# Activations split per head pair, six single-tile chunks and query lows on GpSimd: one change to a fused attention and expert kernel

## Chip, cores and metric

The kernel runs on one core of a Trainium2 chip. The metric is the time of one launch in microseconds (us) on the device: the median of three runs before the change is 1324.6 us.

## The reference

Top-k attention over q, k, v of shape (4, 8, 576, 64), then two expert layers over the 2304 rows of 512 that it leaves. All is float32.

```python
scores = scale * np.matmul(q, k.transpose(0, 1, 3, 2))
kth = np.partition(scores, -32, axis=-1)[..., -32:-31]
scores = np.where(scores >= kth, scores, -1e9)
attn = softmax(scores)                      # over the 32 that are kept
x = (attn @ v) as (2304, 512)
x = (sigmoid(x @ w_gate) * (x @ w_val)) @ w_out     # 512 -> 1536 -> 512
out = relu(x @ w_in) ** 2 @ w_out2                  # 512 -> 2048 -> 512
```

## The kernel before

The 2304 rows are 18 tiles of 128 rows. Attention works on a *unit*: one tile and one head, so 8 units to a tile and 144 in all; a head pair `hp` is two heads of a tile, four pairs to a tile. The expert layers work on *chunks* of one or two tiles (`CHUNKS`, line 30): tiles 0 to 3 alone, then seven pairs. All matrices are wanted at nearly float32 accuracy: the experts' operands are split into a high and a low float16 part and multiplied in three terms; chunk 0 alone (`PLAIN`) is multiplied in float32 while the weights are still being converted.

A unit runs so. `Pair.queries` (302) transposes a pair's queries on TensorE (PE) into PSUM; ScalarE (ACT) copies the high part out and VectorE (DVE) subtracts it to get the low part (line 320). `scores` (325) multiplies them with the keys and ACT copies the result to `S` (347). `softmax` (350) finds the 32 largest of a row with four MAX8 and three MATCH_REPLACE8 on DVE (358, 364), GpSimd (POOL) makes the biases `bs`, and ACT masks and exponentiates. Then there are two ways, parted by `TCI` (65). Chunks below it normalise on POOL, transpose the probabilities on PE (`transpose`, 430) and multiply them with float32 values (`values`, 508). Chunks from it on keep two float16 parts of the probabilities (ACT 386 and 387, POOL 391 and 394), turn them with a transposing DMA (410) and multiply them with float16 values on PE (`values16`, 468). The values for that are prepared once for each batch and head pair: `prep_values` and `split_values` (186, 210) scale them by a power of two, kept in `vsc`, and write them to memory as two parts.

`values16` ends with a float32 product on POOL into the chunk's `xt` (504). When a chunk has all four head pairs, `split_x` (695) takes its norm (ACT square, four matmuls with ones into `pq`, a reduction and `pow2_scale` on DVE), scales it to the high part `xs[0]` on ACT (692) and makes the low part in two POOL passes (701, 702). Only then may the chunk's gate and value matmuls (738) run. They are followed by w_out (778), a second such split (805 to 820), w_in (841) and w_out2 (862).

The weights are converted and split in the first part (`conv`, `split`): the low part of every `LOP`-th block is made on POOL (652, 653), of the others on DVE (650).

The order on each engine is set ahead by a scheduler from priorities and dependences; the engines then run their queues in order. `attend` (1121) emits units ahead of the expert steps, by `LEAD` units for chunks below `PRE0` and by `LEAD2` after it; from `PRE0` on the next chunk's first gate and value blocks (`NPRE`) are put ahead of the present chunk's second layer. Within attention, `head(n + 1)` (1016) emits loads, queries and scores of the next unit, and `tail` (1050) the values of an earlier one. `add_manual_dep` ties an instruction behind another for the order alone.

## Time and profile before

| what | value |
|---|---|
| median of 3 runs | 1324.6 us (1322.24 to 1328.76) |
| the profiled execution | 1327.31 us, of which the span from its first to its last instruction is 1325.5 us |
| PE (matmuls) busy | 1190.7 us, 90% |
| DVE busy | 999.0 us, 75% |
| POOL busy | 809.7 us, 61% |
| ACT busy | 807.8 us, 61% |
| mean granted PE clock | 0.942 of full |

Busy times are unions over the span; PE's contain matmuls whose ends are modelled. The shares are means over a first part with weight conversion and attention, a middle with attention and experts, and an end with experts alone. Tile names in rows are the program's: `S` scores, `W` work copy, `PT` turned probabilities, `xp` the value product, `xs` the parts of x, `qt` queries, `pg`, `pv`, `acc`, `ph` the experts' accumulators.

### The profile page before, as it was taken

To read this page: it belongs to the slowest core of one execution; us is meant where nothing else is said; L and a number is where in the kernel's file an instruction comes from. 1 tells how busy PE (TensorE), PEld (TensorE's weight loads), DVE (VectorE), ACT (ScalarE), POOL (GpSimd) and SP (SyncE) were. 2 spreads that over 40 slices of the span, in tenths; PEclk is the share of its full clock that TensorE was granted. 3 is DMA by queue.
4 is the path that set the end of the run, shared out by engine and by line. 5 is a ranking of instruction groups with operands and counts; after the bars stand their busy time and mean duration, and the time that the engine had idled before them with its cause. 6 is when DMAs were issued, how large, how long until landed. Compare 5 with 4: busy or idle time off the path is not lost.

```text
span 1325.5 us, 30239 instructions
## 1 busy us (share of the span) xinstructions
PE 1190.7 (90%) x11357; PEld 947.1 (71%) x11357; DVE 999.0 (75%) x2040; ACT 807.8 (61%) x1584; POOL 809.7 (61%) x1324
## 2 busy tenths in 40 slices
PE   6756999977989879889986999999999999999998
PEld 5544886865868758756874768877886887787775
DVE  6999996897899989887989777878999899210010
ACT  4777786776666676656666665656677657323122
POOL 1798868867566576557556764575657647424223
PEclk9658999979999979979996999999999999999999
DMA  7988851233356454656745255556444333100000
GB/s 196 330 285 293 269 178 28 77 100 101 102 120 144 115 129 98 147 115 155 179 109 128 72 128 136 123 124 152 100 100 108 97 82 65 44 1 1 17 1 16
DMA packets 263409, 157.95 MB, mean 119 GB/s; under 512 B 213344, under 2 KB 229728, under 8 KB 263264
## 3 DMA queue, kind: packets, MB, share of 16 engines
q1 hardware_dynamic: 263264, 156.03, 45.4%
q8 instruction: 89, 1.46, 0.5%
q14 instruction: 56, 0.46, 0.1%
HBM read 103.55 MB, written 19.40 MB: 93 GB/s over the span
## 4 chain that ended last, share of the span: by engine, by line
PE 54%; POOL 11%; DVE 10%; DMA 8%; ACT 8%; issue 6%; SPq 2%; ACTq 0%; POOLq 0%; DVEq 0%
PE ph L841 12%; PE acc L862 11%; PE pg L738 7%; PE pv L738 6%; PE acc L778 6%; PE sp L344 5%; DMA PT<-S 3%; DVE mx L358 3%; DVE W L364 3%; PE xp L482 3%; POOL S L391 2%; ACT W L387 1%; DMA kst<-ks 1%; ACT W L376 1%; ACT S L386 1%
## 5 line engine op out<-in xcount | busy, mean ns | idle before, releaser
L358 DVE MAX8 mx<-W 128x8 f32<-128x576 f32 x432 | 327.5, 758 | 10.5
L841 PE MATMUL ph<-x,wi_w 128*128 128x256 f16 (+1 forms) x1920 | 207.6, 262 | 7.1 <-ACT x L817 6.3
L364 DVE MATCH_REPLACE8 W<-mx,W 128x576 f32<-128x576 f32 x288 | 213.7, 742 | 0.0
L391 POOL TENSOR_TENSOR S<-W,S 128x512 f16<-128x512 f32 x112 | 130.0, 1160 | 128.7 <-ACT W L387 127.6
L862 PE MATMUL acc<-w_w,rh 128*128 128x512 f16 x816 | 194.8, 380 | 4.0 <-POOL rh L854 4.0
L841 PEld LDWEIGHTS <-wi_w 128*128 128x128 f16 x1920 | 167.9, 100 | 41.5 <-issue 9.9
L376 ACT ACTIVATE W<-S,bs 128x576 f32<-128x576 f32 x144 | 111.6, 775 | 106.7 <-POOL bs L372 106.2
L344 PE MATMUL sp<-kst,qt 128*128 128x288 f32 x608 | 139.2, 337 | 25.7 <-ACT S L347 14.5
L738 PE MATMUL pg<-xs,wg_w 128*128 128x256 f16 (+1 forms) x1440 | 157.7, 261 | 2.8 <-POOL xs L702 2.0
L738 PE MATMUL pv<-xs,wv_w 128*128 128x256 f16 (+1 forms) x1440 | 153.1, 258 | 1.2 <-ACT th L748 0.6
L738 PEld LDWEIGHTS <-wg_w 128*128 128x128 f16 x1440 | 124.6, 99 | 21.4 <-issue 3.7
L862 PEld LDWEIGHTS <-rh 128*128 128x128 f16 x816 | 77.1, 98 | 82.6 <-POOL rh L854 5.9
L347 ACT COPY S<-sp 128x576 f32<-128x576 f32 x144 | 91.6, 636 | 72.9 <-DMA PT<-S 36.3
L778 PEld LDWEIGHTS <-wo_w 128*128 128x128 f16 x1440 | 123.0, 99 | 17.9 <-issue 5.1
L738 PEld LDWEIGHTS <-wv_w 128*128 128x128 f16 x1440 | 123.1, 99 | 16.7 <-issue 3.4
L778 PE MATMUL acc<-gh,wo_w 128*128 128x256 f16 (+1 forms) x1200 | 123.4, 255 | 4.6 <-POOL gh L754 2.8
L344 PEld LDWEIGHTS sp<-kst,qt 128*128 128x128 f32 x608 | 93.6, 196 | 43.7 <-ACT S L347 20.0
L750 DVE TENSOR_TENSOR th<-pv,th 128x512 f32<-128x512 f32 (+1 forms) x60 | 36.2, 604 | 111.4 <-PE pv L738 105.1
L853 POOL TENSOR_TENSOR r<-r 128x512 f32<-128x512 f32 (+1 forms) x80 | 74.5, 932 | 72.7 <-ACT rh L852 66.3
L358 DVE MAX8 mx<-S 128x8 f32<-128x576 f32 x144 | 107.0, 743 | 9.4 <-ACT S L347 9.4
L364 DVE MATCH_REPLACE8 W<-mx,S 128x576 f32<-128x576 f32 x144 | 106.9, 742 | 0.0
L386 ACT ACTIVATE S<-W,bs 128x576 f16<-128x576 f32 x112 | 86.7, 775 | 19.5 <-POOL bs L380 15.7
(336 smaller groups left out, 2172.1 us busy)
## 6 DMA issues: line engine op xcount, KB each, us to landing
kst<-ks SPq DMA_DIRECT2D x104, 288.0 KB, 3.1
v<-vd SPq DMA_DIRECT2D x40, 320.0 KB, 3.2
qn<-in_q_dram SPq DMA_DIRECT2D x128, 64.0 KB, 2.3
wi_r<-in_moe_w_in_dram SPq DMA_DIRECT2D x16, 512.0 KB, 6.6
w_r<-in_moe_w_out_dram SPq DMA_DIRECT2D x16, 512.0 KB, 4.9
wg_r<-in_moe_w_gate_dram SPq DMA_DIRECT2D x12, 512.0 KB, 6.5
wv_r<-in_moe_w_val_dram SPq DMA_DIRECT2D x12, 512.0 KB, 6.9
wo_r<-in_moe_w_out_dram SPq DMA_DIRECT2D x12, 512.0 KB, 6.0
```

Source lines behind the costliest of these rows:

```text
L344: nc.tensor.matmul(sp[:, e, 0:HALF], l, r, start=(x == 0), stop=(x == len(ops) - 1))
L347: nc.scalar.copy(ss.rearrange("p (e s) -> p e s", e=2), sp[:, :, 0:HALF])
L358: m8 = nc.vector.max(mx[:, r], cur)
L364: nc.vector.match_replace(wk, mx[:, r], cur, NEG)
L376: nc.scalar.activation(wk, ss, AF.Prelu, bias=bs[:, 0:1], scale=1.0, alpha=BIG)
L386: nc.scalar.activation(pp[:, 0:S], wk, AF.Exp, bias=bs[:, 1:2], scale=SCALE)
L391: nc.gpsimd.tensor_tensor(pp[:, S + ST : 2 * S], wk[:, 0:SM], pp[:, 0:SM], op=ALU.subtract)
L738: nc.tensor.matmul(pp[:, e * N : (e + 1) * N], wblk(wd, a, c, f0, P), xs[:, b_, c, :], start=(e == 0 and n == 0), stop=(n == 3 * KM - 1), ...
L778: nc.tensor.matmul(acc[:, d // 2, (d % 2) * N : (d % 2 + 1) * N], wblk("wo", a, f, d * P, P), gh[:, b_, e * N : (e + 1) * N], start=(f == ...
L841: nc.tensor.matmul(ph[:, e * N : (e + 1) * N], wblk("wi", a, c, f0, P), x2[:, b_, c, :], start=(e == 0 and n == 0), stop=(n == 3 * KM - 1) ...
L853: nc.gpsimd.tensor_tensor(r, r, r, op=ALU.mult)
L862: nc.tensor.matmul(acc2[:, i, 0:DM], gh[:, b_, e * N + i * P : e * N + (i + 1) * P], wblk("w2", a, f, 0, DM), start=(f == 0 and x == 0), s ...
```

## The change

Tiles 4 and 5 become chunks of their own, so there are twelve chunks, of which six are single; `TCI` is 6, so tiles 4 and 5 now take PE's transposes and float32 values, and batch 0's values are no longer prepared. For chunks from `TCI` on there is no `split_x`: the scale of the values is carried into the normalisation by `xfac`, one factor for each batch and head pair against a common scale of the chunk, and `values16` writes each head pair's product directly as two float16 parts: POOL product, ACT copy, POOL subtraction. The low part of the queries is made by POOL, from a second ACT copy of the transposed queries into `qn`. `LOP` 3 puts eleven of 34 weight lows on POOL where eight were. `LEAD` is 9 for 5, `PRE0` 6 for 5 (the same tiles). For chunks from `TCI` on, the next unit's `head` is emitted behind the present unit's MAX8 rows, without raised priority, and the reciprocal of the sums is tied to the second of them. Keys are prepared together with a batch's values. `ve` moves to another tag, and `mx` has two buffers for three.

```diff
-CHUNKS = [[0], [1], [2], [3]] + [[i, i + 1] for i in range(4, 18, 2)]
+CHUNKS = [[0], [1], [2], [3], [4], [5]] + [[i, i + 1] for i in range(6, 18, 2)]
-LEAD = 5
+LEAD = 9
-PRE0 = 5
+PRE0 = 6
-LOP = 4
+LOP = 3
-TCI = 4
+TCI = 6
...
-        ve = apool.tile([P, 2, D], F32, tag="qn", bufs=2, name=f"ve_{n}")
+        ve = apool.tile([P, 2, D], F32, tag="we", bufs=3, name=f"ve_{n}")
...
+    def xfac(ci, b):
+        if ci not in xfacs:
+            bs_ = batches(ci)
+            vf = vsc.bitcast(F32)
+            ix = mpool.tile([P, 1], F32, tag="xsc", bufs=3, name=f"ix_{ci}")
+            nc.vector.reduce_max(ix, vf[:, bs_[0] * NHP : (bs_[-1] + 1) * NHP, 1], axis=AX.X)
+            nc.gpsimd.tensor_scalar(ix, ix, 2.0, None, op0=ALU.mult)
+            fs = {}
+            for b_ in bs_:
+                f = mpool.tile([P, NHP], F32, tag="xfc", bufs=4, name=f"xfc_{ci}_{b_}")
+                nc.gpsimd.tensor_scalar(
+                    f, vf[:, b_ * NHP : (b_ + 1) * NHP, 0], ix, 1.0, op0=ALU.mult, op1=ALU.mult
+                )
+                fs[b_] = f
+            xfacs[ci] = ix, fs
+        return xfacs[ci][1][b]
...
                     nc.scalar.copy(qt[:, 0, :, sl], p3[:, :, sl])
-                    nc.vector.tensor_tensor(
-                        qt[:, 1, :, sl], p3[:, :, sl], qt[:, 0, :, sl], op=ALU.subtract
+                    whole = qn.rearrange("p j a d -> p j (a d)")[:, :, sl]
+                    nc.scalar.copy(whole, p3[:, :, sl])
+                    nc.gpsimd.tensor_tensor(
+                        qt[:, 1, :, sl], whole, qt[:, 0, :, sl], op=ALU.subtract
                     )
...
-            mx = apool.tile([P, TOPK // 8, 8], F32, tag="mx", bufs=3, name=f"mx_{tt}_{h}")
+            mx = apool.tile([P, TOPK // 8, 8], F32, tag="mx", bufs=2, name=f"mx_{tt}_{h}")
...
-                            vsc.bitcast(F32)[o : o + n, b * NHP + self.hp, 0:1],
+                            xfac(self.ci, b)[o : o + n, self.hp : self.hp + 1],
...
-            nc.gpsimd.tensor_tensor(
-                self.xt[:, self.hp, i * P : (i + 1) * P], xr[:, 0:P], xr[:, P : 2 * P], op=ALU.mult
-            )
+            xf = xr[:, 0:P]
+            nc.gpsimd.tensor_tensor(xf, xf, xr[:, P : 2 * P], op=ALU.mult)
+            hi, lo = (self.xt[:, a, self.hp, i * P : (i + 1) * P] for a in range(2))
+            nc.scalar.copy(hi, xf)
+            nc.gpsimd.tensor_tensor(lo, xf, hi, op=ALU.subtract)
...
+                    if (b, pr.hp) not in done:
+                        done.add((b, pr.hp))
+                        prep_keys(b, pr.hp)
...
-            with tc.high_priority(offset=int(up[0])):
-                head(n + 1)
-                if n > 0 and units[n - 1][0].ci < TCI:
-                    tail(n - 1)
-                if pr.ci >= TCI - 2:
-                    def late(mark, n=n):
-                        while late_values:
-                            split_values(*late_values.pop(0), mark)
-                        if units[n - 2][0].ci >= TCI:
-                            tail(n - 2, mark)
+            if pr.ci < TCI:
+                with tc.high_priority(offset=int(up[0])):
+                    head(n + 1)
+                    if n > 0 and units[n - 1][0].ci < TCI:
+                        tail(n - 1)
+            if pr.ci >= TCI - 2:
+                def late(marks, n=n, pr=pr):
+                    if pr.ci >= TCI:
+                        head(n + 1)
+                        if units[n - 1][0].ci < TCI:
+                            tail(n - 1)
+                    while late_values:
+                        split_values(*late_values.pop(0), marks[3])
+                    if units[n - 2][0].ci >= TCI:
+                        tail(n - 2, marks[3], marks[1])
```

What it does to the order shows best where the chunk of tiles 8 and 9 passes from attention to the experts. On PE before, the last value product `xp_3` is followed by the norm `x_6pq`, the next queries and scores, and only then by the first gate matmul on `xs` (the last number of a name is a buffer's):

```order
L494 MATMUL xp_3_10046<-ident,z_3_9663 64x128 x2
L688 LDWEIGHTS ones
L688 MATMUL x_6pq<-xs_10081,ones 128x256
...
L307 MATMUL qpt_1_10198<-ident,qn_1_9745 128x128 x2
L307 MATMUL qpt_1_10306<-ident,qn_1_9748 128x128 x2
L344 MATMUL sp_2_10335<-kst_2_2_9919,qt_1_2_10201 128x288 x4
L738 LDWEIGHTS wg_w_1877
L738 MATMUL pg_0_10444<-xs_10081,wg_w_1877 128x256
```

On PE now, nine gate and nine value matmuls on the first three head pairs (`xs_9479`), scores and the end of the chunk ahead (`acc_6`) stand before that last value product:

```order
L766 LDWEIGHTS wg_w_1885
L766 MATMUL pg_0_11130<-xs_9479,wg_w_1885 128x256
...
L766 MATMUL pv_0_11131<-xs_9479,wv_w_1895 128x256
L368 MATMUL sp_1_10861<-kst_1_2_10430,qt_0_2_10384 128x288 x4
L766 LDWEIGHTS wv_w_1895
...
L806 LDWEIGHTS wo_w_2023
L806 MATMUL acc_6_10507<-gh_5_10964,wo_w_2023 128x256
L508 LDWEIGHTS v_3_2_9833
L508 MATMUL xp_3_10716<-PT_6_10313,v_3_2_9833 64x128
```

The norm's rows are gone, and the gate matmuls have moved from behind the last head pair to ahead of it.

On DVE before, in the same place, between the MAX8 and MATCH_REPLACE8 rows of a unit:

```order
L364 MATCH_REPLACE W_1_10341<-mx_1_10342,S_1_10191 128x576
L690 TENSOR_REDUCE x_6cm<-x_6pq 128x1
L358 MAX mx_1_10342<-W_1_10341 128x8
L129 TENSOR_SCALAR x_6sn<-x_6cm 128x1
L364 MATCH_REPLACE W_1_10341<-mx_1_10342,W_1_10341 128x576
L132 TENSOR_SCALAR x_6s<-x_6sn 128x1
L135 TENSOR_SCALAR x_6s<-x_6sn 128x1
L320 TENSOR_TENSOR qt_1_2_10201<-qpt_1_10198,qt_1_2_10201 128x256
L358 MAX mx_1_10342<-W_1_10341 128x8
```

On DVE now, the unit whose scores follow the first gate matmuls:

```order
L383 MAX mx_1_10968<-S_1_10860 128x8
L390 MATCH_REPLACE W_1_10967<-mx_1_10968,S_1_10860 128x576
L383 MAX mx_1_10968<-W_1_10967 128x8
L499 RECIPROCAL z_0_10612<-z_0_10612 128x2
L390 MATCH_REPLACE W_1_10967<-mx_1_10968,W_1_10967 128x576
L383 MAX mx_1_10968<-W_1_10967 128x8
```

The reduction, the scale steps and the query lows have left DVE's queue.

On POOL before, the chunk's product is followed by a unit's biases and lows and then by the two passes over the whole chunk:

```order
L504 TENSOR_TENSOR xt_8962<-xr_3_10078 128x128
L372 TENSOR_SCALAR bs_0_10213<-mx_0_10205 128x1
L373 TENSOR_SCALAR bs_0_10213<-mx_0_10205 128x1
L380 TENSOR_SCALAR bs_0_10213<-bs_0_10213 128x1
L391 TENSOR_TENSOR S_0_10030<-W_0_10204,S_0_10030 128x512
L394 TENSOR_TENSOR S_0_10030<-W_0_10204,S_0_10030 128x64
L221 MEMSET voe_2_10848 64x2x64
L701 TENSOR_SCALAR xt_8962<-xt_8962,x_6s 128x1024
L702 TENSOR_TENSOR xs_10081<-xt_8962,xs_10081 128x1024
```

On POOL now, two query lows and a unit's biases stand between the product of the last head pair and its low part:

```order
L531 TENSOR_TENSOR xr_3_10748<-xr_3_10748 128x128
L344 TENSOR_TENSOR qt_1_2_10870<-qn_1_10422,qt_1_2_10870 128x256
L398 TENSOR_SCALAR bs_0_10874<-mx_0_10852 128x1
L399 TENSOR_SCALAR bs_0_10874<-mx_0_10852 128x1
L344 TENSOR_TENSOR qt_1_2_10979<-qn_1_10425,qt_1_2_10979 128x256
L406 TENSOR_SCALAR bs_0_10874<-bs_0_10874 128x1
L534 TENSOR_TENSOR xs_9479<-xr_3_10748,xs_9479 128x128
```

The passes over 1024 columns became one of 128 columns for each head pair and tile, and the query lows came in between.

## Rows read from the trace of the kernel before

**Rows 1.** Page, part 2: busy tenths of an engine in 40 slices.
```profile
PE   6756999977989879889986999999999999999998
DVE  6999996897899989887989777878999899210010
```

**Rows 2.** Windows: length, busy us (instructions) of PE, PEld, DVE, ACT, POOL; clock, DMA, GB/s.
```profile
0.00:361.00 361.00, 288.35 (x2593) 238.94 (x2594) 315.34 (x601) 255.33 (x519) 256.04 (x329) 0.88 0.57 178
361.00:687.00 326.00, 294.38 (x3241) 236.27 (x3240) 286.06 (x612) 214.88 (x441) 202.60 (x405) 0.95 0.57 132
687.00:729.00 42.00, 25.58 (x243) 19.65 (x241) 36.13 (x83) 26.74 (x52) 26.86 (x52) 0.74 0.51 125
729.00:1134.00 405.00, 398.83 (x3813) 311.96 (x3814) 347.56 (x715) 262.65 (x495) 259.89 (x473) 0.99 0.47 106
1134.00:1325.50 191.50, 183.55 (x1475) 140.25 (x1473) 13.94 (x34) 48.17 (x78) 64.25 (x68) 0.99 0.04 12
```

**Rows 3.** Windows of line 358 alone, the MAX8 rows on DVE.
```profile
0.00:361.00 361.00, 93.67 (x129) 0.88 0.57 178
361.00:687.00 326.00, 142.75 (x194) 0.95 0.57 132
687.00:1134.00 447.00, 190.69 (x256) 0.97 0.47 108
```

**Rows 4.** Timeline, 706 to 721 us: start, us, what, [idle before, releaser].
```profile
706.62 0.46 POOL L504 TENSOR_TENSOR xt<-xr 128x128 f32<-128x128 f32 x1
...
708.22 1.01 PE L688 MATMUL x_6pq<-xs,ones 128*128 128x256 bf16 x4 [6.41 <-ACT xs L685]
...
713.22 1.13 POOL L701 TENSOR_SCALAR xt<-xt,x_6s 128x1024 f32<-128x1024 f32 x1
714.43 2.13 POOL L702 TENSOR_TENSOR xs<-xt,xs 128x1024 f16<-128x1024 f32 x1
...
717.99 2.69 PE L738 MATMUL pg<-xs,wg_w 128*128 128x256 f16 x23
```

**Rows 5.** DVE's waits, 0 to 687, then 687 to 1134: us, times, longest.
```profile
DVE qt L320 <- ACT qt L319: 8.5, 7, 3.1
...
DVE qt L320 <- ACT qt L319: 21.6, 12, 7.0
```

**Rows 6.** Groups by shape, whole span: count, busy us, mean ns, idle before.
```profile
L320 DVE TENSOR_TENSOR qt<-qpt,qt 128x256 fp32r<-128x256 f32 x64 | 26.6, 416 | 14.4 <-ACT qt L319 13.8
L650 DVE SCALAR_TENSOR_TENSOR wi_w<-wi_c,wis,wi_w 128x1024 f16<-128x1024 f32 x7 | 12.4, 1770 | 0.4 <-ACT wi_w L647 0.4
L853 POOL TENSOR_TENSOR r<-r 128x256 f32<-128x256 f32 x24 | 16.2, 680 | 4.6 <-ACT rh L852 3.9 <-ACT vs L205 0.2
L482 PE MATMUL xp<-PT,v 128*64 128x64 f16 x448 | 12.0, 199 | 0.0
L482 PE MATMUL xp<-PT,v 128*64 128x128 f16 x1344 | 54.4, 230 | 4.7 <-DMA PT<-S 4.7
L494 PE MATMUL xp<-ident,z 128*64 128x128 f32 x224 | 23.6, 291 | 0.5 <-DVE z L473 0.5
L445 PE MATMUL tp<-ident,W 128*128 128x128 f32 x64 | 11.2, 301 | 2.3 <-POOL W L427 2.2
L518 PE MATMUL xp<-PT,v 128*64 128x128 f32 x256 | 22.6, 333 | 2.4 <-ACT PT L446 2.3
L518 PE MATMUL xp<-PE,v 64*64 64x128 f32 x64 | 8.6, 326 | 0.0
L841 PE MATMUL ph<-x,wi_w 128*128 128x128 f16 x576 | 41.0, 226 | 3.7 <-ACT x L817 3.0 <-ACT r L850 0.8
L841 PE MATMUL ph<-x,wi_w 128*128 128x256 f16 x1344 | 166.6, 278 | 3.3 <-ACT x L817 3.3
```

**Rows 7.** Timelines of PE: w_in matmuls in one go, 128 and 256 columns.
```profile
465.57 1.50 PE L841 MATMUL ph<-x,wi_w 128*128 128x128 f16 x24
...
1195.62 8.02 PE L841 MATMUL ph<-x,wi_w 128*128 128x256 f16 x72
```

More of the change, by code (lines that the diff above doesn't have):

```diff
@@ L253, in tile_topk_attention__then__two_moe_layers @@
     last_max = []
+    xfacs = {}
+    def xfac(ci, b):
[14 more added lines that the diff above has]
+        return xfacs[ci][1][b]
     class Pair:
@@ L354, in softmax @@
             wk = apool.tile([P, S], F32, tag="W", bufs=3, name=f"W_{tt}_{h}")
-            mx = apool.tile([P, TOPK // 8, 8], F32, tag="mx", bufs=3, name=f"mx_{tt}_{h}")
+            mx = apool.tile([P, TOPK // 8, 8], F32, tag="mx", bufs=2, name=f"mx_{tt}_{h}")
             cur = ss
+            marks = []
             for r in range(TOPK // 8):
@@ L362, in softmax @@
                     )
+                marks.append(m8.ins)
                 if r < TOPK // 8 - 1:
@@ L367, in softmax @@
             if late is not None:
-                late(m8.ins)
+                late(marks)
             bs = apool.tile([P, 4], F32, tag="bs", bufs=3, name=f"bs_{tt}_{h}")
@@ L466, in transpose, with values16 @@
                 nc.scalar.copy(self.pe[:, i * P : (i + 1) * P], tq[:, 0:P])
-        def values16(self, i, after=None):
+        def values16(self, i, after=None, summed=None):
             tt = self.tts[i]
@@ L473, in values16 @@
             rc = nc.vector.reciprocal(z, z)
-            if after is not None:
-                tc.add_manual_dep(rc.ins, after.name, NOSYNC, reason="summed by then")
+            if summed is not None:
+                tc.add_manual_dep(rc.ins, summed.name, NOSYNC, reason="summed by then")
             terms = [(a, c, c) for c in range(CB + 1) for a in range(2)]
@@ L1048, in head, with tail @@
                 nxt.queries(nxt.tts[0:1])
-        def tail(n, after=None):
+        def tail(n, after=None, summed=None):
             pr, pi, j, i = units[n]
@@ L1054, in tail @@
             if pr.hp == 0 and pr.ci not in xts:
-                if pr.ci in XP:
+                if pr.ci >= TCI:
+                    xts[pr.ci] = mpool.tile(
+                        [P, 2, KM, pr.N], F16, tag="m4", bufs=M4, name=f"xs_{pr.ci}"
+                    )
+                elif pr.ci in XP:
                     if not plain:
@@ L1073, in tail @@
             if pr.ci >= TCI:
-                pr.values16(i, after)
+                pr.values16(i, after, summed)
             else:
@@ L1080, in tail @@
                 if pr.hp == NHP - 1:
-                    xsp[pr.ci] = pr.xt if pr.ci in PLAIN else split_x(pr.ci, pr.xt)
+                    if pr.ci in PLAIN:
+                        xsp[pr.ci] = pr.xt
+                    elif pr.ci < TCI:
+                        xsp[pr.ci] = split_x(pr.ci, pr.xt)
+                    else:
+                        xsp[pr.ci] = pr.xt, xfacs[pr.ci][0]
         head(0)
@@ L1085, in attention @@
             late = None
-            with tc.high_priority(offset=int(up[0])):
-                head(n + 1)
-                if n > 0 and units[n - 1][0].ci < TCI:
-                    tail(n - 1)
-                if pr.ci >= TCI - 2:
-                    def late(mark, n=n):
-                        while late_values:
-                            split_values(*late_values.pop(0), mark)
-                        if units[n - 2][0].ci >= TCI:
-                            tail(n - 2, mark)
+            if pr.ci < TCI:
[5 more added lines that the diff above has]
+                def late(marks, n=n, pr=pr):
+                    if pr.ci >= TCI:
+                        head(n + 1)
[5 more added lines that the diff above has]
+                        tail(n - 2, marks[3], marks[1])
             work[n] = pr.softmax(j, i, ready.pop(n), late)
```

## Prediction

> **What bounds the kernel now.** I read the page's slices first, then the windows, then single waits and prices. In the slices VectorE (DVE) stands at 7 to 9 tenths until slice 34 of 40, at 9 mostly in the first 14, and falls to 0 to 2 after it, while TensorE (PE) has its holes in the first 22 slices and is full afterwards [rows 1]. The windows give this in microseconds [rows 2]. The attention of a 128-row tile is 8 heads ("units") of four MAX8 and three MATCH_REPLACE8 on DVE, in order. The MAX8 rows, four to a unit (129, 194 and 256, those on a bound counted twice), put the end of unit 32 (tiles 0 to 3) at 361 us, of unit 80 (tiles 0 to 9) at 687, of unit 144, the last, at 1134 [rows 3]. From 0 to 361 DVE is busy 315.34 of 361. From 361 to 729 PE is busy 294.38 + 25.58 = 320 of 368 and DVE 286.06 + 36.13 = 322: both short of full, each now and then waiting for the other's unit. From 729 to 1134 PE is busy 398.83 of 405, and from 1134 on, with attention over, 183.55 of 191.5. So the span is the time to about 729, which the attention units set, and then PE's remaining work. A microsecond taken off DVE before 729 can count; one taken off after it counts only if PE is less full than it looks. Work added to PE is free only in the holes before 729, 48 us from 361 on.
>
> The last hole shows how the two meet. The last product of chunk 6 (tiles 8 and 9) is on GpSimd (POOL) at 706.62; PE then stands 6.41 us until 708.22, when the norm of x (four matmuls, x_6pq) may start; the second half of x is subtracted from 714.43 to 716.56, and the gate matmuls run in earnest from 717.99 [rows 4]. That is 11 us from the product to the work that uses it.
>
> **The change part by part.** Instruction counts are from the two orders, prices from the trace.
>
> *Up to unit 32 (0 to 361).* The query lows leave DVE: 18 of 80 subtractions stand here, at 0.416 us [rows 6], 7.5 us. Their waits for ScalarE (ACT) are 8.5 us up to 687 and 21.6 after it [rows 5]; I count them in the next stretch. Of the weight lows (L650) three fewer stay on DVE, at 1.77 us [rows 6], 5.3 us. Together -13. POOL takes 18 subtractions at 0.68 (the 128x256 row of L853, POOL's nearest [rows 6]) and three weight lows, two passes over 1024 columns each, which at 1.13 and 2.13 us for passes of that size [rows 4] are 9.8 us; +22 us, and loses the preparation of batch 0's values, which the later switch makes needless; that work is of the same order, so I cost POOL's trade at nothing. Its cover is POOL's idle time, 361 - 256 = 105 us [rows 2]; if POOL is what DVE waits for, the -13 becomes 0. In the other direction, waits that go with the value preparation could add some 10. Bounds -23 to 0; taken -13, since DVE's own busy time is the tightest row of this stretch.
>
> *PE work added.* Tiles 4 and 5 go back from transposing DMAs to PE transposes and float32 values. The price of a PE record is its group's busy time over its count, since the mean of one holds the overlap. Removed, for four head pairs: 4 x (56 x 27 ns + 28 x 40 ns) of values (12.0 us / 448 and 54.4 / 1344) and 32 records of z at 105 ns, 13.9 us. Added: 64 transposes and 8 for the ends, at 175 ns, and values of 64 x 88 ns + 16 x 134 ns = 7.8 us for tile 5, the same to twice that for tile 4, which lies across two batches [rows 6]. That is 28 to 36 us, net 14 to 22; I take 15, because those rows ran between stalls and at a granted clock under 1. Splitting chunk [4, 5] doubles 624 matmuls at half the columns. Back to back, 24 of 128 columns take 1.50 us and 72 of 256 take 8.02 [rows 7]; less one matmul's own length, that is 56 and 109 ns, so 2 x 56 - 109 = 3 ns each, 2 us. The average of the single chunks, 41.0 / 576 = 71 ns [rows 6], stalls included, gives, with 166.6 / 1344 = 124 ns for the halves together, 624 x (142 - 124) = 11 us, the upper bound. The norm matmuls of x go for the six paired chunks and one is added (20 fewer, -2). Sum +15, bounds +14 to +31.
>
> The Trainium skill, "TensorE: Matmul & The Clock Gate", section "Back-to-back issue gap", says that a stream of weight load and matmul pairs runs at about 81 ns for 128 columns, not at the isolated 56. By it the split would cost 624 x 162 ns less 68 us, an estimated 33 us. The 56 ns of the row speaks against it.
>
> *Where the PE work stands.* With LEAD 9 in place of 5, expert rows move behind attention rows. Counting matmuls ahead of unit 32's scores: gate and value 528 before, 288 now; w_out 217 and 144; w_in 192 and 140; 512-column ones 48 and 18. At 56, 56, 56 and 216 ns this takes 27 us of PE work out of the first stretch, where DVE sets the pace. Behind unit 80's scores 57 gate and value and 35 w_out matmuls of 256 columns more stand than before, 92 x 109 ns = 10 us, less the 2 us of norms: +8. The stretch between gets 15 + 27 - 8 = +34.
>
> *Units 32 to 80 and the hole after them (361 to 729).* PE: 320 + 34 = 354. DVE: 322 less 28 subtractions (11.6 us), plus some 8 us of reciprocals, smaller Tanh products and scales moved here, less some 7 of the 8.5 us of waits. So PE becomes the longer one, and the stretch cannot be much under 354. The norm chain (ACT square, four matmuls, a reduction and three scale steps among DVE's MAX8s, ACT copy, two POOL passes, the last 2.13 us) is gone for paired chunks; instead each head pair's product is copied by ACT and subtracted by POOL, 0.46 us, as it comes. In the order the gate matmuls of the first three head pairs now stand ahead of the last pair's values, so PE has work where it stood 6.41 us. With fuller PE the granted clock, 0.95 and 0.74 here [rows 2], should rise: 354 x 0.95 = 336 is the lower bound. The upper one is all 48 us of idle time kept, 402. I take 354: the clock regained pays for the idle that stays. 354 - 368 = -14, bounds -32 to +34.
>
> *After 729.* PE is full, so the DVE's relief there (34 subtractions, 21.6 us of waits) costs and gives nothing; +8 of PE work. Between 0 and +10.
>
> Covered edits, at nothing: ACT's second query copy (80) and the copies of the high parts (48), for which ACT's idle time, over a quarter of every window [rows 2], is the cover; the tile buffers (mx 2, ve under another tag) change no data that is waited for, and if they did, DVE's first MAX8 of a unit would be late.
>
> Sum: -13 - 14 + 8 = **-19**. The profiled execution took 1327.3 us (span 1325.5), the median of the runs is 1324.6, so 1324.6 - 19 = **1306**.
>
> **Rivals.**
> *A, slower.* The holes between 361 and 729 are not lack of work but latency: a unit's chain from the last MAX8 over POOL, ACT, POOL and the transposing DMA to the value matmuls, on which in-order PE stands. POOL's and ACT's shares in this stretch rise by some 30 us each, by the order's counts, since the query lows and the normalisation of tiles 4 and 5 queue there, and the scores of the next pair wait for them. Then PE's 34 us come on top of its idle time: -13 + 34 + 8 = +29, 1354. It turns to slower once the stretch grows by more than 5 us, that is when less than 29 of the 48 us of holes are used; with 14 used it is -13 + 20 + 8 = +15, 1340, which I take as its time. Against it: the longest of those holes, 6.41 us [rows 4], was the norm's, which goes.
> *B, no change.* The first stretch gives nothing, because POOL's lows take the place of DVE's: -14 + 8 = -6, 1319.
> *C, faster still.* PE after 729 is not truly full. The Trainium skill, "Perfetto Trace Analysis", section "Identifying the Most-Contended Engine", says that matmul busy time is a poor measure and that weight-load busy time is better. In rows: PEld is busy 311.96 of 405 there [rows 2]. If the hidden slack is 5%, half of DVE's relief there (34 x 0.416 + 21.6 = 36 us) counts: 1306 - 18 = 1288. Against it: 72 matmuls in 8.02 us are at full pace.
> *D.* The added PE work costs its upper bounds, because weight loads do not hide under 128 columns and values of tile 4 do not shrink with their columns: 31 in place of 15, 1322. The sentence of the Trainium skill quoted above is of this kind; by its figure alone the time would be an estimated 1337.
>
> **How the numbers follow.** Forecast 0.50, its own range 1294 to 1318; A 0.17; B 0.15; C 0.12; D 0.06. The range leaves out at most two in ten: down to C's side, 1284, up to short of A's full price, 1336. Half a per cent, about what a measurement of this kernel can tell, is 1318 to 1331. Faster: forecast 0.47, C 0.12, of B 0.03, of A none, 0.62. Same: forecast 0.03, B 0.12, D 0.05, 0.20. Slower: A and the rest, 0.18.
>
> **What would show it.** Right: unit 32 ends near 348, unit 80 at 660 to 675, PE idle between there and the last unit near nothing, and the tail behind the last unit longer by 10 to 20 us, as more expert work stands there. The stretch to unit 32 unchanged would speak for B; a PE idle of 40 us or more in units 32 to 80 with POOL or transposing DMAs as releaser for A; MAX8s that end earlier while the total falls by the same for C; 128-column rows over 65 ns for D. The step I trust least is that PE's added 34 us find the holes.

## Result and profile after

The kernel after takes 1305.4 us (median of four runs) beside 1325.3 us of the kernel before on the same chip: ratio 0.9847 [0.9817, 0.9876], 20 us faster. The forecast was 1306. Below, "before" took 1330 to 1331 us on the chips of the experiments, so kernels are compared by their ratio to it; 0.001 is 1.3 us. On one of those chips the kernel after itself stood at 0.9827 [0.9808, 0.9846].

The profiled execution took 1302.8 us, of which 1301.0 are span. The page's slices of it answer to [rows 1]:

```profile
PE   6756989878999898998988999999999999999998
DVE  6999989999759978799879779999999976010010
```

The windows of after, cut at its own unit ends (unit 32 at 331, 40 at 403, 48 at 451, 80 at 670.5, 144 at 1100.5), have the columns of [rows 2]:

```profile
0.00:331.00 331.00, 259.90 (x2151) 211.21 (x2152) 306.26 (x551) 240.47 (x472) 249.53 (x301) 0.85 0.56 180
331.00:403.00 72.00, 68.96 (x943) 60.23 (x942) 48.56 (x119) 45.97 (x121) 45.93 (x100) 0.98 0.49 135
403.00:451.00 48.00, 46.29 (x651) 41.05 (x649) 46.48 (x105) 34.32 (x81) 27.70 (x65) 1.00 0.36 98
451.00:670.50 219.50, 202.43 (x2556) 168.89 (x2554) 188.94 (x402) 152.31 (x354) 155.71 (x326) 0.96 0.58 131
670.50:712.00 41.50, 36.13 (x366) 30.48 (x367) 32.77 (x71) 27.51 (x60) 24.11 (x49) 0.96 0.66 154
712.00:1100.50 388.50, 379.31 (x3718) 297.70 (x3716) 342.49 (x683) 267.60 (x549) 284.08 (x542) 1.00 0.49 109
1100.50:1301.00 200.50, 192.32 (x1532) 145.80 (x1529) 12.78 (x27) 48.54 (x80) 65.25 (x71) 0.99 0.04 12
```

Set against [rows 2], stretch by stretch:

| stretch | before | after | change | forecast |
|---|---|---|---|---|
| up to unit 32 | 361.0 | 331.0 | -30 | -13 |
| units 32 to 80 and the 42 us behind | 368.0 | 381.0 | +13 | -14 |
| from there to the end | 596.5 | 589.0 | -7.5 | +8 |
| span | 1325.5 | 1301.0 | -24.5 | -19 |

So the total is right and none of its three terms is: the errors cancel, by luck. Two questions follow: what took 30 us out of the first stretch, when the edits that the forecast priced there are worth 13; and what became of the middle.

**The first stretch.** DVE's busy time fell by 9 us (315.3 to 306.3) and its idle time by 21 (45.7 to 24.7). Most of the loss before sits in one tile: tile 2 (units 16 to 24) holds 18.1 us of this idle time before and 3.6 after. The rest is in tile 3 (12.1 against 4.5), where before prepares batch 1's values. Tile 2 in the windows of before:

```profile
192.30:299.10 106.80, 94.03 (x983) 77.09 (x983) 88.67 (x154) 77.54 (x150) 82.83 (x103) 0.92 0.25 67
```

and in those of after:

```profile
199.60:272.60 73.00, 66.59 (x693) 53.70 (x691) 69.42 (x119) 55.16 (x99) 63.53 (x78) 0.98 0.24 63
```

Of the 106.8 us before, one unit took 32.8. Its timeline in the kernel before (start, us, engine, line, operation; rows of the other engines between):

```profile
185.68 0.63 ACT L201 ACTIVATE vom<-vm 128x512 bf16<-128x512 f32 x1
...
206.43 0.73 DVE L358 MAX8 mx<-S 128x8 f32<-128x576 f32 x1
207.09 3.18 DVE L650 SCALAR_TENSOR_TENSOR wg_w<-wg_c,wgs,wg_w 128x1024 f16<-128x1024 f32 x1
207.60 0.63 ACT L201 ACTIVATE vom<-vm 128x512 bf16<-128x512 f32 x1
...
214.06 1.77 POOL L427 TENSOR_SCALAR W<-W,rz 128x512 f32<-128x512 f32 x1
...
229.72 0.17 PE L213 MATMUL vn<-vs,ones 128*128 128x1 bf16 x1
229.75 0.63 PE L445 MATMUL tp<-ident,W 128*128 128x128 f32 x4
230.80 1.28 DVE L650 SCALAR_TENSOR_TENSOR wo_w<-wo_c,wos,wo_w 128x1024 f16<-128x1024 f32 x1 [5.54 <-ACT wo_w L647]
232.07 0.74 DVE L364 MATCH_REPLACE8 W<-mx,S 128x576 f32<-128x576 f32 x1
...
236.98 0.37 SPq L228 DMA_DIRECT2D vd<-vom  x1
```

The unit's first MAX8 ends at 207.2 and its first MATCH_REPLACE8, the first instruction that writes a `W` tile, starts 24.9 us later. There are three `W` buffers, and the value preparation takes its tile `vom` from them. One is held from 185.68, when the squares of batch 0's first head pair are written, until its parts have been sent to memory from 236.98 on; a second from 207.60, for the second head pair; the third still holds the probabilities of the unit before, which PE turns at 229.75 to 230.4. They had been ready since 215.8: PE's queue had expert rows of chunk 0 and the preparation's own norm matmul (L213) ahead of the transposes. In the five kernels of the table below that prepare values in tile 2, unit 16's transposes start 6.8 to 13.9 us after their input is ready, and in the three that do not 0.2 to 3.6. So the preparation may hold the unit up in two ways, by the buffers and by the order in PE's queue, and no run parts the two. DVE's queue has weight lows in the gap, and they wait in their turn for ACT. The two longest waits of DVE up to unit 32 (us, times, longest) are these:

```profile
DVE wo_w L650 <- ACT wo_w L647: 9.8, 3, 5.5
DVE W L364 <- DMA vd<-vom: 7.5, 4, 3.8
```

In after batch 0's values are not prepared, and nothing of the kind stands there.

### The profile page after: what moved, and what is told of

The parts are those of the page before. It is cut to its first block, busy times and chain, and to the rows that moved or that the text cites. A ratio compares the mean times of both kernels' runs of the same rounds, so it can differ in the third digit from the quotient of the medians.

```text
span 1301.0 us, 31666 instructions
## 1 busy us (share of the span) xinstructions
PE 1185.3 (91%) x11901; PEld 955.4 (73%) x11901; DVE 978.3 (75%) x1954; ACT 816.7 (63%) x1714; POOL 852.3 (66%) x1450
## 4 chain that ended last, share of the span: by engine, by line
PE 55%; DVE 12%; POOL 11%; DMA 8%; ACT 6%; issue 5%; SPq 2%; POOLq 0%; ACTq 0%; DVEq 0%
PE ph L869 11%; PE acc L890 10%; PE pv L766 7%; PE pg L766 7%; PE acc L806 7%; PE sp L368 5%; DVE mx L383 4%; DVE W L390 3%; DMA PT<-S 3%; POOL S L417 2%; PE xp L508 2%; PE xp L546 2%; DMA wg_r<-in_moe_w_gate_dram 2%; POOL rh L882 1%; ACT W L413 1%
## 5 line engine op out<-in xcount | busy, mean ns | idle before, releaser
L869 PE MATMUL ph<-x,wi_w 128*128 128x256 f16 (+1 forms) x2112 | 210.6, 254 | 9.5 <-ACT x L845 8.3
L869 PEld LDWEIGHTS <-wi_w 128*128 128x128 f16 x2112 | 172.9, 100 | 40.7 <-issue 11.6
L417 POOL TENSOR_TENSOR S<-W,S 128x512 f16<-128x512 f32 x96 | 111.3, 1159 | 80.2 <-ACT W L413 79.2
L778 DVE TENSOR_TENSOR th<-pv,th 128x512 f32<-128x512 f32 (+1 forms) x66 | 37.1, 562 | 137.6 <-PE pv L766 126.5
L806 PEld LDWEIGHTS <-wo_w 128*128 128x128 f16 x1584 | 127.5, 99 | 14.2 <-issue 2.0
L806 PE MATMUL acc<-gh,wo_w 128*128 128x128 f16 (+1 forms) x1344 | 126.1, 247 | 0.8 <-POOL gh L782 0.6
L882 POOL TENSOR_TENSOR rh<-r,rh 128x512 f16<-128x512 f32 (+1 forms) x88 | 83.3, 948 | 4.2
```

The source lines that it names most:

```text
L417: nc.gpsimd.tensor_tensor(pp[:, S + ST : 2 * S], wk[:, 0:SM], pp[:, 0:SM], op=ALU.subtract)
L806: nc.tensor.matmul(acc[:, d // 2, (d % 2) * N : (d % 2 + 1) * N], wblk("wo", a, f, d * P, P), gh[:, b_, e * N : (e + 1) * N], start=(f == ...
L869: nc.tensor.matmul(ph[:, e * N : (e + 1) * N], wblk("wi", a, c, f0, P), x2[:, b_, c, :], start=(e == 0 and n == 0), stop=(n == 3 * KM - 1) ...
L882: nc.gpsimd.tensor_tensor(gh[:, 1], r, gh[:, 0], op=ALU.subtract)
```

## Experiments

The waits above give a number that can be read in every kernel: the time from the end of a unit's first MAX8 to the start of its first MATCH_REPLACE8, summed over the eight units of tile 2 (worked out from the timelines).

| kernel | values prepared in tile 2 | that time, us | unit 32 ends | ratio to before |
|---|---|---|---|---|
| before | yes | 42.1 | 361 | 1 |
| after | no | 10.5 | 331 | 0.9847 |
| d3_before_tci6 | no | 9.3 | 326 | 0.9868 |
| a1_qdve | no | 8.0 | 324 | 0.9818 |
| a2_prep0 | yes | 32.2 | 355 | 1.0078 |
| d2_prep_veqn | yes | 30.1 | 357 | 1.0029 |
| d1_prep_qdve | yes | 39.9 | 345 | 1.0040 |
| c1_tci4 | yes | 39.3 | 375 | 1.0033 |

DVE runs other rows in part of that time. Its idle time within it is 17.2 us in before, 15.9 to 24.0 in the four other kernels with the preparation in tile 2, and 0.1 to 1.3 in the three without.

**Batch 0's values prepared again (a2_prep0).** The kernel after with that work added in tile 2, as before; nothing reads its result.

```diff
+                if pr.ci == 2:
+                    prep_values(0, pr.hp)
                 if pr.ci == TCI - 2:
...
-            if pr.ci >= TCI - 2:
+            if pr.ci >= 2:
```

> The changed kernel with work added: the values of batch 0 are prepared during chunk 2, as in the kernel before, and nothing uses them. Theory 1, made from the two traces: of the 30 us by which unit 32 ends earlier, some 20 are waits of DVE that this preparation had caused (work buffers held until its transfers had landed, 7.5 us; weight lows waiting for ACT while it squared values, 9.8 us). Then unit 32 ends at 343 to 352 and the total rises by 8 to 18 us, to 1314 to 1323. Rival: the 30 us are the low parts that left DVE, and the preparation was hidden; then unit 32 stays within 5 us of 331 and the total within 4 us of 1305.

Measured: 1.0078 [1.0063, 1.0093]; four preparations cost over 30 us and eat the whole gain, nearly twice what was expected for the dearest case. Which of its sides costs it, POOL's load, a shared buffer, or the order, was open; two runs try the first two.

**The remainder in other buffers (d2_prep_veqn).** After moved `ve` to the tag `we`, which `voe` uses too; here it is in `qn` again, with the preparation in tile 2.

```diff
-        ve = apool.tile([P, 2, D], F32, tag="we", bufs=3, name=f"ve_{n}")
+        ve = apool.tile([P, 2, D], F32, tag="qn", bufs=2, name=f"ve_{n}")
```

> The changed kernel with batch 0's values prepared again during tile 2 as in the run before, the query lows on POOL, and the remainder tile ve in the buffers of the queries, as it was before the change, in place of the three that it shares with the halves voe, which wait there for their own write to memory (4.5 us of ACT's waits in tile 2). If that sharing is the price: ratio 0.985 to 0.995 and ACT's wait on the write gone. If the preparation's work and the order that it forces are the price: ratio 1.003 to 1.012, as with the shared buffers.

Measured: 1.0029 [1.0012, 1.0046]. The sharing costs 6 us, the preparation itself still some 27. The 6 us lie behind unit 80 (`ve` moves for every batch); unit 32 ends no earlier (357 against 355). Tile 2 of this kernel:

```profile
212.20:304.10 91.90, 67.99 (x695) 55.47 (x693) 71.81 (x132) 63.84 (x122) 74.57 (x99) 0.87 0.28 73
```

Beside after's 73.0 us there are 2.4 us more of DVE, 8.7 of ACT and 11.0 of POOL, and 18.9 more on the clock, with each of PE, DVE, ACT and POOL idle for over 17: waiting, not load.

**Preparation with the query lows on DVE (d1_prep_qdve).** If POOL were overfull by the two together, it would have room here.

> The changed kernel with batch 0's values prepared again during tile 2, in units 16 to 24 (added work whose result nothing reads), and the query lows back on DVE. The preparation alone, with the lows on POOL, cost 33 us against the changed kernel's ratio of 0.982; the lows on DVE alone cost nothing. Theory 1 (POOL is what both need: each is free alone, together they overfill it): with the lows on DVE the preparation costs 10 us at most, ratio 0.983 to 0.990, unit 32 at 328 to 340 us. Theory 2 (the preparation costs by its waits and the buffers that it holds, wherever the lows are): ratio 1.000 to 1.010, unit 32 at 345 to 358.

Measured: 1.0040 [1.0023, 1.0056], unit 32 at 345. The second theory holds: the first stretch loses 21 us against a1_qdve, the kernel with the lows on DVE alone, and lost 24 and 26 with the lows on POOL, so POOL's load is at most a small part of the price. In these three kernels the waits of a MATCH_REPLACE8 that name a transfer of `vom` or `voe` come to 1.5 to 1.9 us only, so how the buffers share the price with the order and with the rows queued ahead stays open.

**One part of the change on the kernel before (d3_before_tci6).**

```diff
-CHUNKS = [[0], [1], [2], [3]] + [[i, i + 1] for i in range(4, 18, 2)]
+CHUNKS = [[0], [1], [2], [3], [4], [5]] + [[i, i + 1] for i in range(6, 18, 2)]
-PRE0 = 5
+PRE0 = 6
-TCI = 4
+TCI = 6
```

> The kernel before with one part of the change alone: tiles 4 and 5 as chunks of their own that take PE's transposes, TCI and PRE0 6, so that batch 0's values are not prepared; LEAD, LOP, query lows, float32 x and its split as before. Theory 1 (the preparation in stretch 1 is what the change gets rid of, 28 us when it is undone): ratio 0.978 to 0.988, unit 32 at 335 to 345 us. Theory 2 (the parts need one another: without LEAD 9 and the direct split PE's added 15 us find no room): ratio 0.993 to 1.003.

Measured: 0.9868 [0.9844, 0.9893], 17.5 us of the 20 to 24. Its windows:

```profile
0.00:325.70 325.70, 263.21 (x2311) 218.24 (x2312) 306.03 (x574) 239.93 (x462) 231.40 (x282) 0.90 0.58 184
...
325.70:674.00 348.30, 318.02 (x4116) 272.14 (x4114) 289.97 (x654) 225.53 (x513) 208.88 (x443) 0.98 0.50 125
674.00:716.00 42.00, 25.48 (x204) 20.39 (x204) 34.27 (x78) 25.74 (x51) 25.85 (x51) 0.58 0.54 119
716.00:1123.00 407.00, 399.55 (x3840) 312.72 (x3839) 350.33 (x722) 265.28 (x497) 259.64 (x474) 0.99 0.47 106
```

The first stretch loses 35 us, units 32 to 80 take 22 of them back, and from unit 80 on it is the kernel before again: 42 us with PE busy for 25.5, then 407. What the other parts of the change gain, they gain from unit 32 on.

**The reverse (c1_tci4).** The kernel after with `TCI` 4 and its six single chunks kept.

```diff
-TCI = 6
+TCI = 4
```

> The changed kernel with TCI 4: tiles 4 and 5 stay single chunks but turn their probabilities by DMA and multiply float16 values again, so batch 0's values are prepared in the first part. Two effects of TCI 6 come apart here. Theory 1 (the preparation in the first part is what cost the time): unit 32 ends at 345 to 360, and since PE loses some 15 us of work behind it, unit 80 at 670 to 690; total 10 to 20 us above the changed kernel. Rival (moving tiles 4 and 5 to PE's transposes is a loss of its own, which hides a gain elsewhere): unit 32 within 8 us of 331 and the total 5 to 15 us below the changed kernel.

Measured: 1.0033 [1.0013, 1.0052]. Units 32 to 80 are shorter by 14 us (327 against 341.6 on that chip), with tiles 4 and 5 on the transposing DMAs and batch 1's preparation gone from there; the preparations, of batch 0 in tile 2 and of batch 1 in tile 3 as in before, lengthen the first stretch by 45 (375 against 330). Together, all other parts of the change without this one are worth nothing; up to 6 us of that may be `ve`, which shares its buffers here as in a2_prep0.

**Query lows back on DVE (a1_qdve).**

```diff
-                    whole = qn.rearrange("p j a d -> p j (a d)")[:, :, sl]
-                    nc.scalar.copy(whole, p3[:, :, sl])
-                    nc.gpsimd.tensor_tensor(
-                        qt[:, 1, :, sl], whole, qt[:, 0, :, sl], op=ALU.subtract
+                    nc.vector.tensor_tensor(
+                        qt[:, 1, :, sl], p3[:, :, sl], qt[:, 0, :, sl], op=ALU.subtract
                     )
```

> The changed kernel with one part undone: the query lows are subtracted by DVE from PSUM again, and the second ACT copy goes. By the account of the prediction (DVE's own time counts up to unit 32 and hardly after it) unit 32 ends 7 to 10 us later than in the changed kernel, near 340, and the total is 8 to 15 us above it, 1313 to 1320. The rival, that DVE's relief counts over the whole span (80 subtractions at 0.4 us and some 30 us of waits for ACT), gives 1335 to 1360. A third, that POOL's added load costs as much as DVE gains, gives 1300 to 1308.

Measured: 0.9818 [0.9794, 0.9841], the same as after (0.9827 and 0.9847 with theirs). Moving the 80 subtractions off DVE is worth nothing, as the third theory had it. Unit 32 even ends 7 us earlier with them on DVE (324 against 331), a lead that is nearly gone at unit 144 (1099 against 1100.5), and the first stretch shows why. The weight conversion's line 635 (633 in this kernel), 68 rows on DVE with two inputs from memory on the chip; the window of that line alone (length, busy us of DVE, clock, DMA share, GB/s) in after:

```profile
0.00:331.00 331.00, 56.31 (x68) 0.85 0.56 180
```

and in a1_qdve:

```profile
0.00:324.00 324.00, 49.46 (x68) 0.88 0.58 184
```

The same 68 rows take 6.9 us more with the lows on POOL; the 23 weight lows of line 678 take 37.1 against 35.4. That is 8.5 us given back for the 7.5 that the 18 subtractions freed. In the other direction, the stretch from unit 80's passage to unit 144 is as long here, with 8.3 us more on DVE (after is the window from 712 above):

```profile
708.80:1099.00 390.20, 379.04 (x3700) 297.13 (x3699) 350.79 (x715) 260.86 (x516) 261.95 (x507) 0.99 0.48 108
```

**LOP 4 and LOP 2 (c2_lop4, d4_lop2).** Eight, and 17, of the 34 weight lows on POOL in place of 11.

> The changed kernel with LOP 4: three weight lows go back from GpSimd to DVE. By the prediction's sum unit 32 ends 4 to 6 us later and the total is 3 to 6 us higher. Rival, after the query lows turned out to move nothing: GpSimd holds the first part as much as DVE, so unit 32 is within 3 us and the total within 4 us of the changed kernel.

> The changed kernel with LOP 2: 17 of 34 weight lows on POOL in place of 11, 6 fewer on DVE at 1.77 us, 10.6 us off DVE, 20 us more on POOL, in the first stretch. From 4 to 3 the step was worth 6.5 us for three lows. If DVE still sets the pace up to unit 32: 6 to 12 us faster than the changed kernel, ratio 0.973 to 0.978, unit 32 at 319 to 325. If POOL, at 250 of 331 us busy and ahead of DVE's reciprocals and PE's transposes, is full enough: ratio 0.982 to 0.990, unit 32 at 331 to 340.

Measured: LOP 4 0.9876 [0.9859, 0.9893] and LOP 2 0.9883 [0.9857, 0.9908], both some 7 us behind LOP 3. Three lows off DVE pay 6.5 us in all, where 5.3 were priced, but in the first stretch only 3: unit 32 ends at 333.3 with LOP 4 and at 330.4 in after on that chip. Six more do not pay, although DVE is busy for 5.8 us less:

```profile
0.00:332.40 332.40, 260.77 (x2122) 210.97 (x2123) 300.50 (x545) 241.42 (x471) 260.57 (x308) 0.84 0.57 181
```

Unit 32 ends no earlier (332 against 331), and units 32 to 80 take 347 us in place of 340; through which wait was not followed up.

**LEAD 5 (a3_lead5).**

```diff
-LEAD = 9
+LEAD = 5
```

> The changed kernel with LEAD 5 as before. In the changed kernel PE is idle 71 us up to unit 32 and busy 318 of 339.5 us from there to unit 80. If the 27 us of expert work that LEAD 9 moved out of the first part would fit into its idle time, this is faster by 10 to 20 us, 1285 to 1295, with unit 32 still near 331 and unit 80 at 650 to 660. Rival: the moved expert steps bring their DVE, ACT and POOL work with them and hold attention up in the first part by as much as they give back later: unit 32 at 340 to 350, total 1302 to 1312.

Measured: 0.9924 [0.9909, 0.9939], 13 us slower than after and slower than either theory said.

```profile
0.00:335.70 335.70, 264.95 (x2301) 215.59 (x2301) 308.74 (x553) 241.58 (x476) 253.19 (x306) 0.87 0.56 177
335.70:692.30 356.60, 327.89 (x4134) 277.26 (x4134) 285.86 (x626) 234.65 (x557) 231.00 (x489) 0.97 0.49 123
692.30:734.30 42.00, 31.06 (x253) 24.04 (x254) 34.13 (x76) 26.76 (x57) 23.18 (x50) 0.68 0.66 153
```

LEAD takes only 5 us of PE work out of the first stretch (264.95 against 259.90). What it gives stands between units 32 and 80: 357 us here, 340 in after. In the 42 us behind unit 80 PE is idle for 10.9 us here, for 5.4 in after.

**Float32 x and its split restored (a4_xnorm)**, for the chunks from `TCI` on, with the scale back in the normalisation.

```diff
-            xf = xr[:, 0:P]
-            nc.gpsimd.tensor_tensor(xf, xf, xr[:, P : 2 * P], op=ALU.mult)
-            hi, lo = (self.xt[:, a, self.hp, i * P : (i + 1) * P] for a in range(2))
-            nc.scalar.copy(hi, xf)
-            nc.gpsimd.tensor_tensor(lo, xf, hi, op=ALU.subtract)
+            nc.gpsimd.tensor_tensor(
+                self.xt[:, self.hp, i * P : (i + 1) * P], xr[:, 0:P], xr[:, P : 2 * P], op=ALU.mult
+            )
```

> The changed kernel with one part undone: chunks from the seventh on write float32 x and split it with its norm when the chunk is complete, as before. If PE's stand at the passage from attention to experts was the norm's (16 us idle in 42 us before, 5 us now), the holes come back at the first passages, and 24 norm matmuls (2.6 us) on full PE: 1312 to 1322, PE's idle time between units 80 and 86 over 12 us. Rival: the hole was lack of attention results, and is smaller now only because PE has more to do there: 1304 to 1309.

Measured: 0.9877 [0.9861, 0.9894], 7 us slower than after. The total lies in the first theory's range, but its mark is missing: PE is idle for 9.0 us between units 80 and 86, not for over 12, and for 7.7 in the 42 us behind unit 80, where before has 16.4:

```profile
669.30:711.30 42.00, 34.27 (x332) 27.68 (x330) 29.74 (x69) 27.23 (x56) 26.37 (x50) 0.88 0.64 154
```

So the norm made little of that hole.

**The next unit's scores emitted early again (c3_headearly)**, beside the kernel after itself (c0_same) on the same chip.

```diff
-            if pr.ci < TCI:
-                with tc.high_priority(offset=int(up[0])):
-                    head(n + 1)
-                    if n > 0 and units[n - 1][0].ci < TCI:
-                        tail(n - 1)
+            with tc.high_priority(offset=int(up[0])):
+                head(n + 1)
+                if n > 0 and units[n - 1][0].ci < TCI:
+                    tail(n - 1)
```

> The changed kernel with the next unit's loads, queries and scores emitted ahead of the present unit's MAX8 rows for all chunks, as before. The prediction gave this part no term: within 4 us of the changed kernel, with the units past 48 ending within 6 us of it. Rival: the later place keeps PE's and ACT's queues free for the experts, and without it the stretch from unit 48 to the end is longer by 10 us or more.

> The changed kernel as it is, to have it on the same chip as the runs beside it: a ratio to the kernel before of 0.982 to 0.988 by every theory, and unit 32 at 328 to 334, unit 80 at 666 to 674.

Measured: 0.9892 [0.9871, 0.9914] against 0.9827: the place of `head` alone is worth 9 us, for which the prediction had no term. Both this and the direct split pay behind unit 80. The stretch from the passage to unit 144, in the windows of c3_headearly:

```profile
714.50:1117.60 403.10, 389.18 (x3717) 302.89 (x3716) 343.88 (x686) 269.73 (x549) 282.09 (x540) 0.97 0.46 105
```

of a4_xnorm:

```profile
711.30:1116.00 404.70, 395.97 (x3826) 309.08 (x3827) 346.46 (x699) 272.19 (x532) 283.28 (x513) 1.00 0.46 105
```

and of c0_same:

```profile
714.00:1105.00 391.00, 381.54 (x3722) 299.19 (x3720) 342.76 (x683) 268.04 (x550) 284.41 (x542) 1.00 0.49 109
```

With the early head some 3720 matmuls take 12 us longer, in 4.5 us more of idle time and 7.6 more of busy time, at a granted clock of 0.97 for 1.00. With float32 x there are 104 matmuls more in the stretch and 48 fewer behind it, where the tail is 8 us shorter, and 5 us remain, of PE's busy time and not of idle time.

Undone one at a time, the parts are worth 27 (c1_tci4), 13 (a3_lead5), 9 (c3_headearly), 7 (a4_xnorm), 7 (c2_lop4) and 0 us (a1_qdve), together far more than the 20 to 24 of all. So they are not independent: chunks and `TCI` give 17.5 by themselves (d3_before_tci6), the others together give nothing without them and some 3 to 6 with them. No other part was tried by itself on the kernel before.

## Why the prediction was right, step by step

**Up to unit 32, -13 said, -30 measured: the step that failed.** The -13 was made of query lows (7.5) and weight lows (5.3). The second gives 3 in this stretch (c2_lop4). The first is wrong in sign here: unit 32 ends 7 us later with the lows on POOL (a1_qdve). And the value preparation, whose going I set off against POOL's new work "at nothing", with "some 10" as the most its waits could add, is worth about 27 in the total by itself (d2_prep_veqn), and with batch 1's, which moves from tile 3 to tile 4, 35 in the first stretch of d3_before_tci6; the other parts of the change give 5 of these back. I had set its instructions (some 9 us of ACT and 11 of POOL by d2_prep_veqn) against POOL's new work, and not what waits behind it. The bound of -23 was broken for the same reason. That the preparation in tile 2 is the cause is shown by the five kernels of the table with it and the three without; that it acts through the `W` buffers, through PE's queue or both is read from the timeline and its waits. No run gave it buffers of its own or another place in PE's queue.

**PE work.** The chunk split was said to cost 2 us, at most 11: the busy times of the gate, value, w_out and w_in groups sum to 670 before and 677 after, +7. Tiles 4 and 5 were said to cost 15 with the norms, and the groups of after say less:

```profile
L869 PE MATMUL ph<-x,wi_w 128*128 128x128 f16 x960 | 69.7, 229 | 6.2 <-ACT x L845 6.2
L508 PE MATMUL xp<-PT,v 128*64 128x128 f16 x1232 | 47.1, 223 | 0.0
L546 PE MATMUL xp<-PT,v 128*64 128x128 f32 x320 | 23.7, 294 | 1.6 <-ACT PT L472 1.6
L471 PE MATMUL tp<-ident,W 128*128 128x128 f32 x128 | 21.6, 294 | 6.3 <-POOL W L453 6.3
```

Against [rows 6] the transposes added 10.4 us, about as priced (64 at 175 ns are 11.2), but the float32 values of line 546 went from 88 ns each to 74 (320 in 23.7 us), so that all the rows added come to 24 us and those removed to 18: +6. PE's busy time as a whole was to grow by 15 and fell by 5 (1190.7 to 1185.3); the granted clock, 0.950 for 0.942, would make some 10 of that as an estimate.

**PE work moved, 27 us out of the first stretch: right in size (28.5), wrong in its cause.** LEAD moves 5 of it. The rest moves in d3_before_tci6 too, whose LEAD is 5: PE is busy there for 263 us where it was 288 [rows 2]. With unit 32 earlier by 35 us, less expert work stands ahead of it.

**Units 32 to 80, -14 said, +13 measured.** PE's busy time is what was forecast, 353.8 for 354, but by luck: of the terms +15, +27 and -8 the runs show -5 for all added work, +28.5 from the first stretch and +10.7 from behind. What failed is "the clock regained pays for the idle that stays": the clock rose (0.74 to 0.96 in the passage), and yet of the 48 us of holes 27 stayed. In the passage the order went as described. In after:

```profile
695.99 0.45 POOL L531 TENSOR_TENSOR xr<-xr 128x128 f32<-128x128 f32 x1
...
697.19 0.66 PE L368 MATMUL sp<-kst,qt 128*128 128x288 f32 x3 [1.58 <-POOL qt L344]
...
698.67 0.42 POOL L534 TENSOR_TENSOR xs<-xr,xs 128x128 f16<-128x128 f32 x1
699.14 1.03 PE L766 MATMUL pg<-xs,wg_w 128*128 128x256 f16 x8 [1.06 <-POOL xs L534]
```

From the last product to the gate matmul that needs it are 3.2 us where there were 11 [rows 4], and PE's idle time in these 42 us fell from 16.4 to 5.4. That was not the norm alone, as the prediction had it. The 6.41 us of idle PE that it gave to the norm [rows 4] end at 708.22, so they began at 701.81, 4.8 us before the last product: for most of them PE stood at the norm's matmul, but for the head pair's result. With the norm back (a4_xnorm) 7.7 us are left, with LEAD 5 and no norm (a3_lead5) 10.9, and with the norm, LEAD 5 and the early head (d3_before_tci6) 16.5. The holes that stayed are in the paired chunks between 451 and 670 (17 of the 27). In tile 4 PE is full (68.96 of 72 us): there the value preparation of batch 1 stands now, the first MATCH_REPLACE8s are late by 26 us in all, and PE is idle for 3.0 us all the same, since it has expert rows to run meanwhile.

**After that, +8 said, -7.5 measured.** PE's busy time from unit 80 to the end is 608 us in both kernels, so no work was added; 10.5 us of it have moved into the passage, and the stretches behind hold as much less, which shortens them by 7.5. The 10 us that the prediction counted from unit 80's scores on are of this size, but the passage, which it put into the stretch before, starts there. The prediction had the direct split in the passage alone, and the later head nowhere.

**Rivals.** A: in size it was right for the middle, which grew by 13 us, with 21 of the 48 us of holes used. It saw the total turn slower below 29; the total is faster all the same, because the first stretch gave more than twice what I had said. Its mechanism is not shown. Its mark, 40 us or more of idle PE in units 32 to 80 with POOL or the transposing DMAs as releasers, is missing: 21.8 us are idle there, and PE's longest waits from 331 to 712 are for the second split of x, key loads and the preparation's norms:

```profile
PE ph L869 <- ACT x L845: 6.0, 3, 3.5
PE kpt L164 <- DMA kn<-in_k_dram: 4.4, 3, 2.3
PE vn L213 <- ACT vs L205: 3.8, 2, 2.5
```

No wait for a transposing DMA is among the 13 kinds that the view lists there; from 361 to 729 before, such waits came to 4.7 us. B: falls, unit 32 ends 30 us earlier, though its suspicion of the query lows was right. C: falls; putting 34 rows back on DVE behind unit 80 changes nothing there (a1_qdve). The Trainium skill, "Perfetto Trace Analysis", section "Identifying the Most-Contended Engine", says to judge TensorE's headroom by the share of its peak work that is done or by weight-load busy time, and not by matmul busy time. Weight loads are busy for 297.7 of 388.5 us there, and yet DVE's relief does not count. D: the split cost 7 us where its price was 11. Its mark, 128-column rows over 65 ns, was ill chosen: they are at 73 (69.7 / 960), but were at 71 before [rows 6], since the mean holds stalls. In one go they run as before, 24 in 1.50 us, or 56 ns each once one matmul's own length is taken off:

```profile
348.27 1.50 PE L766 MATMUL pg<-xs,wg_w 128*128 128x128 f16 x24
```

The 81 ns of the Trainium skill, "TensorE: Matmul & The Clock Gate", section "Back-to-back issue gap", are not seen in either kernel.

Of the marks set, unit 80 (660 to 675 said, 670.5) fits, unit 32 (348 said, 331) does not, and the tail grew by 9 us where 10 to 20 were said.

## What to carry to other kernels

Price a side job not by its instructions alone but by what has to wait behind it, in the main loop's buffers and in each engine's queue: here four jobs of some 22 us of engine time in all cost 27 us, while they held work buffers of the main loop, and the first stood ahead of its transposes on PE. Which of the two counts for how much is not shown. Such a job costs less where another engine has work of its own to run meanwhile; in tile 4, where PE was full, the preparation of batch 1 left PE idle for 3 us. And when a sum of terms comes out right, look at the terms: these were off by 17, 27 and 15 us in both directions.

## What the runs showed of the hardware

Some DVE rows lengthen beside POOL work, and MAX8 and MATCH_REPLACE8 do not. Line 635's rows (128x512, two inputs from on-chip memory) took, in after, 0.67 us as a mean of the 13 that had POOL idle for over nine tenths of their time, 0.91 of the 53 that had it busy for over half, and up to 1.80. Line 634's rows (128x1024, one input) took 0.69 us (4 rows) and 1.13 us (29 rows) in the same two cases, MAX8 up to unit 32 0.756 and 0.750 us (15 and 104 rows), and MATCH_REPLACE8 0.742 and 0.740 (8 and 78). With the query lows back on DVE line 635's rows took 6.9 us less in all. So in this kernel a row that is handed from DVE to POOL is paid for in part by the DVE rows that stay.
